# GeGLU feed-forward, first loads: x by quarters of D, the first two tiles of the weight chunk ahead of the others on two queues, four banks held instead of six

## The chip, the cores and the metric

One core of one Trainium2 chip. The metric is device time in microseconds (us), from several executions of each kernel. TensorE does the matmuls and transposes and writes them to PSUM, which this kernel uses as eight banks; ACT and DVE copy the results on; loads are issued on the queues of SP and of ACT.

## The reference

```python
B, S, D, F = 1, 2048, 1024, 3584      # bf16
def reference(x, w_gate, w_up, w_down):
    return (gelu_tanh(x @ w_gate) * (x @ w_up)) @ w_down
```

## The kernel before

The kernel keeps all weights' chunks and activations in SBUF and works in phases: a start phase of plain units for the first chunk of four tiles (128 bf16 matmuls of 128x512), then pairs of tiles with a seven-product scheme (12.6 us a pair), then the down projection, and the pairs and the down projection once more for the second half of the rows. The change concerns the start phase alone: how the first 512 rows of x and the first chunk of w_gate and w_up get in, and in which order TensorE uses them.

```python
    XQ = 512
    NXQ = D // XQ
    KPQ = XQ // P
    WKP = 2
    NSU = 3
    NWARM = 11
# ...
    def load_w(key, k0, k1, eng):
        c0 = key[1] * FG
        for w_sb, wv in zip(chunks[key], (wgv, wuv)):
            i = eng.dma_start(out=w_sb[:, k0:k1, :], in_=wv[:, k0:k1, c0 : c0 + FG])
            if eng is nc.sync:
                sp(i)
# ...
    new_chunk((0, 0))
    load_x0_piece(0)
    load_w((0, 0), 0, WKP, nc.scalar)
    nc.scalar.preload_act_table(ACT.Gelu_apprx_tanh)
    ident = const_pool.tile([P, P], BF16, name="ident")
    make_identity(nc, ident[:])

    warm_l = nc.const_aps.tensor(1.0, [P, P], BF16)
    warm_r = nc.const_aps.tensor(1.0, [P, TB], BF16)
    warm = []
    for i in range(NWARM):
        b = banks[i % 8]
        warm.append(
            nc.tensor.matmul(b[:], lhsT=warm_l, rhs=warm_r, start=True, stop=True)
        )

    load_x0_piece(1)
    for k0 in range(WKP, KD, WKP):
        load_w((0, 0), k0, k0 + WKP, nc.sync)
    load_xT(xT, 0, 1, 0, KD)
    new_chunk((0, 1))
    load_w((0, 1), 0, KD, nc.sync)
# ...
    def first_units(hT):
        groups = [warm, transpose_x_piece(0)]
        held = [(banks[2 + 2 * u], banks[3 + 2 * u]) for u in range(NSU)]
        bank_ctr[0] = 0
        for kd in range(KD):
            if kd == KPQ - 1:
                bank_ctr[0] = 0
                groups.append(transpose_x_piece(1))
            g = []
            for j, w_sb in enumerate(chunks[(0, 0)]):
                g += [mm_gu(held[u][j], w_sb, u, 0, kd) for u in range(NSU)]
            groups.append(g)
        for ga, gb in zip(groups[:-1], groups[1:]):
            tc.add_manual_dep(
                gb[0].ins, ga[-1].ins.name, SCHED_DEP, reason="startup PE order"
            )
        t_sum("t1")
        for u in range(NSU):
            mult(hT, gelu(held[u][0]), held[u][1], u, 0)
```

In words: x's first block comes as two halves of 512 columns on the SP queue; the first gate and up rows come on the ACT queue, the rest on SP. TensorE fills the time with eleven matmuls on constants, transposes one half of x, works on three tiles at once (six PSUM banks held), transposes the other half and goes on. `on`, `sp`, `act`, `dve`, `pe` are helpers that fix the order of instructions on an engine.

Of the kernel before, what the change touches and what calls it, by code (L numbers as in the profile page):

```python
# [8 lines left out]
ACT = mybir.ActivationFunctionType  # L9
# [25 lines left out]
def kernel(  # L35
# [23 lines left out]
    DN = 512  # L59
    NDN = D // DN  # L60
    TSB = TB // P
    XQ = 512
    NXQ = D // XQ
    KPQ = XQ // P
    WKP = 2
    NSU = 3
    NWARM = 11
    NPAIR = KF // 2
    PPG = FPG // 2
    WDT = 2  # L70
# [36 lines left out]

    banks = [psum.tile([P, TB], F32, name=f"bank{i}") for i in range(8)]
    PB, VB, QB, RB = (0, 1), (2, 3), (4, 5), (6, 7)
    bank_ctr = [0]  # L110

    def next_bank():
        b = banks[bank_ctr[0] % 8]
        bank_ctr[0] += 1
        return b

    last_on = {}

    def on(engine, inst):
# [8 lines left out]
    def sp(inst):  # L128
        return on("sp", inst)

    def act(inst):
        return on("act", inst)

    def dve(inst):
        return on("dve", inst)
# [12 lines left out]
    def pe(inst):  # L148
        return on("pe", inst)
# [11 lines left out]
            for j in range(2)  # L161
        )

    def load_w(key, k0, k1, eng):
        c0 = key[1] * FG
        for w_sb, wv in zip(chunks[key], (wgv, wuv)):
            i = eng.dma_start(out=w_sb[:, k0:k1, :], in_=wv[:, k0:k1, c0 : c0 + FG])  # L167
            if eng is nc.sync:
                sp(i)

    def load_x0_piece(q):
        sp(
            nc.sync.dma_start(
                out=xs0[:, :, q * XQ : (q + 1) * XQ],
                in_=x2[0:TB, q * XQ : (q + 1) * XQ].rearrange(
                    "(ts p) d -> p ts d", p=P
                ),
            )
        )

    def load_xT(xT, h, tb, k0, k1):
        t0 = h * SH + tb * TB
# [6 lines left out]

    xT = xT_pool.tile([P, KD, SH], BF16, name="xT")  # L190
    new_chunk((0, 0))
    load_x0_piece(0)
    load_w((0, 0), 0, WKP, nc.scalar)
    nc.scalar.preload_act_table(ACT.Gelu_apprx_tanh)
    ident = const_pool.tile([P, P], BF16, name="ident")
    make_identity(nc, ident[:])

    warm_l = nc.const_aps.tensor(1.0, [P, P], BF16)
    warm_r = nc.const_aps.tensor(1.0, [P, TB], BF16)
    warm = []  # L200
    for i in range(NWARM):
        b = banks[i % 8]
        warm.append(
            nc.tensor.matmul(b[:], lhsT=warm_l, rhs=warm_r, start=True, stop=True)
        )

    load_x0_piece(1)
    for k0 in range(WKP, KD, WKP):
        load_w((0, 0), k0, k0 + WKP, nc.sync)
    load_xT(xT, 0, 1, 0, KD)  # L210
    new_chunk((0, 1))
    load_w((0, 1), 0, KD, nc.sync)


    tsum = {}
# [25 lines left out]


    def mm_gu(ps, w_sb, fi, tb, kd):
        return nc.tensor.matmul(  # L244
            ps[:],
            lhsT=w_sb[:, kd, fi * P : (fi + 1) * P],
            rhs=xT[:, kd, tb * TB : (tb + 1) * TB],
            start=(kd == 0),
            stop=(kd == KD - 1),
        )  # L250

    g_ctr = [0]
# [19 lines left out]
            )  # L272
        )

    def unit(hT, key, fi, tb):
        pss = (next_bank(), next_bank())
        for ps, w_sb in zip(pss, chunks[key]):
            for kd in range(KD):
                mm_gu(ps, w_sb, fi, tb, kd)
        mult(hT, gelu(pss[0]), pss[1], key[1] * FPG + fi, tb)  # L280

    evac_ctr = [0]

    def evac(dst, src):
        if evac_ctr[0] % 2 == 0:
            dve(nc.vector.tensor_copy(out=dst, in_=src))
        else:
            act(nc.scalar.copy(out=dst, in_=src))
        evac_ctr[0] += 1

    def transpose_x_piece(q):
        kds = list(range(q * KPQ, (q + 1) * KPQ))
        parts = []
        if q == 0:
            parts = [([kds[0]], (0, 2)), ([kds[0]], (2, 4)), ([kds[1]], (0, 4))]
            kds = kds[2:]
        parts += [(kds[i : i + 2], (0, 4)) for i in range(0, len(kds), 2)]
        insts = []
        for kd_list, (ts0, ts1) in parts:
            n = (ts1 - ts0) * P  # L300
            tp = next_bank()[:].bitcast(BF16)
            for j, kd in enumerate(kd_list):
                for ts in range(ts0, ts1):
                    c = j * n + (ts - ts0) * P
                    insts.append(
                        nc.tensor.transpose(  # L306
                            tp[:, c : c + P],
                            xs0[:, ts, kd * P : (kd + 1) * P],
                            ident[:],
                        )  # L310
                    )
            k0 = kd_list[0]
            evac(
                xT[:, k0 : k0 + len(kd_list), ts0 * P : ts1 * P],
                tp[:, 0 : len(kd_list) * n].rearrange("p (a b) -> p a b", b=n),
            )
        return insts

    def first_units(hT):
        groups = [warm, transpose_x_piece(0)]  # L320
        held = [(banks[2 + 2 * u], banks[3 + 2 * u]) for u in range(NSU)]
        bank_ctr[0] = 0
        for kd in range(KD):
            if kd == KPQ - 1:
                bank_ctr[0] = 0
                groups.append(transpose_x_piece(1))
            g = []
            for j, w_sb in enumerate(chunks[(0, 0)]):
                g += [mm_gu(held[u][j], w_sb, u, 0, kd) for u in range(NSU)]
            groups.append(g)  # L330
        for ga, gb in zip(groups[:-1], groups[1:]):
            tc.add_manual_dep(
                gb[0].ins, ga[-1].ins.name, SCHED_DEP, reason="startup PE order"
            )
        t_sum("t1")
        for u in range(NSU):
            mult(hT, gelu(held[u][0]), held[u][1], u, 0)
        bank_ctr[0] = 0


    ssum = {}
# [434 lines left out]
    for h in range(NH):  # L776
        hT = hT_pool.tile([P, KF, SH], BF16, name="hT")
        first_pair = 0
        if h == 0:
            first_units(hT)  # L780
            t_sum("t2")
            for fi in range(NSU, FPG):
                unit(hT, (0, 0), fi, 0)
            t_sum("b22")
            t_sum("t3")
            unit(hT, (0, 0), 0, 1)
            for name in S_NAMES:
                for j in range(2):
                    s_sum(0, PPG, j, name)
            t_sum("t4")  # L790
            for fi in range(1, FPG):
                unit(hT, (0, 0), fi, 1)
            first_pair = PPG
            xs = [(tb, kd) for tb in range(NTB) for kd in range(KD)]
            stage_load(0)
            stage_load(1)
        for pair in range(first_pair, NPAIR):
            if pair % PPG == 0 and (pair // PPG + 1) * PPG < NPAIR:
                key = (h, pair // PPG + 1)
                if key not in chunks:  # L800
                    new_chunk(key)
                    load_w(key, 0, KD, nc.sync)
            then = {}
            if h == 0:

# [44 lines left out]
        if h + 1 < NH:  # L850
# [7 lines left out]
            def w_fill(c, j):  # L858
                if j == 0:
                    new_chunk((nh, c))  # L860
                w_sb, wv = chunks[(nh, c)][j], (wgv, wuv)[j]
                for k0 in range(0, KD, KH):
                    src = wv[:, k0 : k0 + KH, c * FG : (c + 1) * FG]
                    sp(nc.sync.dma_start(out=w_sb[:, k0 : k0 + KH, :], in_=src))

            def s_fill(j, *names):
                for name in names:
# [60 lines left out]
```

## Time and profile before

| | before |
|---|---|
| median of the first three runs | 545.26 us (544.74 to 545.34) |
| span of the profiled run | 542.7 us |
| TensorE busy | 537.7 us, 99% |
| DVE, ACT, POOL busy | 64%, 48%, 45% |
| first useful instruction on TensorE (transpose) | 5.51 us |
| pairs start | 35.53 us |

How to read it: the list of TensorE's waits has none after 7.65 us, so the end is the start of the pairs plus 507.2 us. Two readings carry everything below. One is "transposes start": the first TensorE instruction that isn't a matmul on constants. The other is "pairs start": the first matmul of the line that holds the pairs' products (L396 in the kernel before, L380 in the changed one). Both are starts as the timeline gives them; from one execution to another of the same kernel they move by up to 0.2 us (e1, e9). A busy share says little here: the constants count as busy.

Two reading aids. The first is the pace of the array, read from the weight loads (PEld). In the kernel before, the loads of the constants start at 3.71, 4.14 and 4.57 us, 0.43 us apart; from 11.95 us on, 110 matmuls of 512 columns take 23.74 us, 0.22 each. "Half rate" and "full rate" stand here for these two paces, and "the switch" for the moment between them. The granted-clock column says 1.00 at both, also in the first 4 us. "Clock" is the word for this pace. The second: the lines of the two kernels have other numbers (L204 and L197 are the constants, L306 and L295 the transposes, L244 and L245 the units).

### The profile page before, as it was taken

The page shows a single profiled execution, that of the slowest core. Times are in us where ns is not written, and L with a number is a line of the kernel's source. Part 1 is how long each engine was busy: PE and PEld are TensorE (multiplying, and loading weights), DVE is VectorE, ACT ScalarE, POOL GpSimd, SP SyncE. Part 2 cuts the span into 40 slices and gives each one's busy share as a digit, 9 for nine tenths or more (in the row PEclk, how much of TensorE's full clock was granted, in tenths as well). Part 3 has the DMA queues.
Part 4 walks back from the last instruction along what each step waited for, and adds up shares of the span by engine and source line. Part 5 has one row for each costly group of instructions (what it writes and reads, how often), then busy time and mean ns, then how long its engine had stood idle before and what let it go on. Part 6 is the DMA issues. An engine that isn't in the chain of part 4 may idle for free.

```text
span 542.7 us, 7261 instructions
## 1 busy us (share of the span) xinstructions
PE 537.7 (99%) x2411; PEld 374.1 (69%) x2411; DVE 349.5 (64%) x465; ACT 259.8 (48%) x434; POOL 242.2 (45%) x206
## 2 busy tenths in 40 slices
PE   8999999999999999999999999999999999999997
PEld 4456677777767676767777766777766776866865
DVE  1826666778766899789484444444454469979961
ACT  2435555555555318216455555555555552462270
POOL 0577777888877000000038776677777630000000
PEclk9999999999999999999999999999999999999999
DMA  9845598877736979679962240404040457767845
GB/s 275 267 133 155 162 241 278 216 252 194 252 137 213 335 246 367 215 245 307 320 213 80 76 129 27 155 2 156 0 156 0 156 171 238 251 219 246 289 146 206
DMA packets 81669, 104.82 MB, mean 193 GB/s; under 512 B 16608, under 2 KB 63200, under 8 KB 81632
## 3 DMA queue, kind: packets, MB, share of 16 engines
q1 hardware_dynamic: 81088, 103.83, 60.0%
q10 hardware_dynamic: 544, 0.52, 0.3%
q8 instruction: 20, 0.33, 0.2%
q14 instruction: 17, 0.14, 0.1%
HBM read 87.56 MB, written 13.63 MB: 186 GB/s over the span
## 4 chain that ended last, share of the span: by engine, by line
PE 98%; DMA 1%; ACT 0%; ACTq 0%; issue 0%
PE bank L396 60%; PE bank L632 32%; PE bank L244 5%; DMA w_mem<-in_w_up_dram 1%; PE bank L306 0%; ACT o_sb L680 0%; ACTq L167 0%; ACTq L680 0%
## 5 line engine op out<-in xcount | busy, mean ns | idle before, releaser
L396 PE MATMUL bank<-t_mem,s_mem 128*128 128x512 f32 x1016 | 249.2, 399 | 0.0
L396 PEld LDWEIGHTS bank<-t_mem,s_mem 128*128 128x128 f32 x1016 | 190.9, 188 | 44.2
L370 POOL TENSOR_TENSOR s_mem<-w_mem 128x512 fp32r<-128x512 bf16 x100 | 120.9, 1230 | 196.1 <-DVE t_mem L238 105.0
L632 PE MATMUL bank<-t_mem,s_mem 128*128 128x512 f32 x560 | 130.1, 392 | 0.0
L419 DVE TENSOR_TENSOR bank<-bank,m 128x512 f32<-128x512 f32 x104 | 72.3, 699 | 81.3 <-ACT bank L439 72.3
L632 PEld LDWEIGHTS bank<-t_mem,s_mem 128*128 128x128 f32 x560 | 105.2, 188 | 22.7
L267 DVE TENSOR_TENSOR hT<-w_mem,bank 128x512 bf16<-128x512 f32 x104 | 71.3, 688 | 54.4 <-ACT w_mem L262 24.6
L262 ACT ACTIVATE w_mem<-bank 128x512 f32<-128x512 f32 x104 | 61.9, 597 | 79.4 <-DVE bank L419 46.2
L396 PE MATMUL bank<-xT,w_mem 128*128 128x512 bf16 x416 | 99.0, 380 | 0.0
L396 PEld LDWEIGHTS <-w_mem 128*128 128x128 bf16 x416 | 36.6, 98 | 50.5 <-issue 13.6
L545 DVE TENSOR_TENSOR t_mem<-w_mem 128x1024 fp32r<-128x1024 bf16 x56 | 65.5, 1216 | 0.0
L370 POOL TENSOR_TENSOR s_mem<-w_mem,s_mem 128x512 fp32r<-128x512 bf16 x50 | 63.3, 1288 | 0.0
L370 POOL TENSOR_TENSOR s_mem<-s_mem,w_mem 128x512 fp32r<-128x512 f32 x50 | 59.3, 1206 | 0.0
L607 DVE TENSOR_TENSOR s_mem<-hT 128x512 fp32r<-128x512 bf16 x56 | 40.5, 754 | 10.5 <-PE bank L632 7.0
L383 ACT CAST s_mem<-w_mem 128x512 fp32r<-128x512 bf16 x52 | 31.9, 615 | 30.4 <-PE bank L396 29.2
L632 PEld LDWEIGHTS <-hT 128*128 128x128 bf16 x224 | 21.3, 98 | 26.6 <-issue 1.8
L434 ACT COPY m<-bank 128x512 f32<-128x512 f32 x52 | 30.6, 589 | 17.2 <-PE bank L396 17.0
L439 ACT COPY bank<-bank 128x512 f32<-128x512 f32 x52 | 29.6, 570 | 17.1 <-PE bank L396 17.1
L430 ACT COPY bank<-bank 128x512 f32<-128x512 f32 x52 | 29.5, 570 | 13.4 <-PE bank L396 13.4
L680 ACT CAST o_sb<-bank 128x512 bf16<-128x512 f32 x28 | 15.4, 586 | 39.6 <-PE bank L632 39.6
L244 PE MATMUL bank<-xT,w_mem 128*128 128x512 bf16 x128 | 28.1, 379 | 0.4 <-DMA w_mem<-in_w_up_dram 0.4
L542 ACT CAST t_mem<-w_mem 128x1024 fp32r<-128x1024 bf16 x28 | 26.9, 1048 | 0.0
(39 smaller groups left out, 233.4 us busy)
## 6 DMA issues: line engine op xcount, KB each, us to landing
t_mem<-t_dram SPq DMA_DIRECT2D x56, 512.0 KB, 5.5
w_mem<-in_w_gate_dram SPq DMA_DIRECT2D x11, 1024.0 KB, 6.2
w_mem<-in_w_up_dram SPq DMA_DIRECT2D x11, 1024.0 KB, 8.4
wd_sb<-in_w_down_dram SPq DMA_DIRECT2D x28, 256.0 KB, 3.4
t_dram<-o_sb SPq DMA_DIRECT2D x28, 256.0 KB, 2.5
wd_sb<-in_w_down_dram SPq DMA_DIRECT2D x12, 512.0 KB, 8.5
w_mem<-in_w_down_dram SPq DMA_DIRECT2D x10, 512.0 KB, 5.8
w_mem<-in_w_down_dram SPq DMA_DIRECT2D x4, 1024.0 KB, 6.8
```

The source lines that it names most:

```text
L244: return nc.tensor.matmul(ps[:], lhsT=w_sb[:, kd, fi * P : (fi + 1) * P], rhs=xT[:, kd, tb * TB : (tb + 1) * TB], start=(kd == 0), stop=(k ...
L262: act(nc.scalar.activation(out=g_sb, in_=ps[:], func=ACT.Gelu_apprx_tanh))
L267: nc.vector.tensor_tensor(out=hT[:, fc, tb * TB : (tb + 1) * TB], in0=g_sb, in1=ps[:], op=ALU.mult,)
L370: pool(nc.gpsimd.tensor_tensor(out=t, in0=in0, in1=in1, op=op))
L383: act(nc.scalar.copy(out=t, in_=a(1, 1)))
L396: nc.tensor.matmul(banks[bank][:], lhsT=lhs[:, c, :], rhs=rhs[:, c, :], start=start and c == 0, stop=c == KH - 1, skip_group_check=True,)
L419: nc.vector.tensor_tensor(out=banks[dst][:], in0=banks[src][:], in1=m5[j][:], op=ALU.add)
L434: act(nc.scalar.copy(out=m5[j][:], in_=banks[VB[j]][:]))
L439: act(nc.scalar.copy(out=banks[RB[j]][:], in_=banks[QB[j]][:]))
L545: dve(nc.vector.tensor_tensor(out=t, in0=in0, in1=in1, op=ALU.subtract))
L607: dve(nc.vector.tensor_tensor(out=t, in0=in0, in1=in1, op=op))
L632: nc.tensor.matmul(banks[bset[u]][:], lhsT=lhs(i, u), rhs=rhs(i), start=start and i == 0, stop=stop and i == NS - 1, skip_group_check=True,)
```

## The change

The intent: get TensorE to useful work earlier by making what the first transposes and matmuls need small, and by letting the rest follow at the pace of the work. Cut to its core:

```diff
-    XQ = 512
+    XQ = 256
     NXQ = D // XQ
     KPQ = XQ // P
     WKP = 2
-    NSU = 3
-    NWARM = 11
+    NWARM = 8
...
-    def load_w(key, k0, k1, eng):
+    def load_w(key, j, k0, k1, queue=sp, f0=0, f1=FG):
+
         c0 = key[1] * FG
-        for w_sb, wv in zip(chunks[key], (wgv, wuv)):
-            i = eng.dma_start(out=w_sb[:, k0:k1, :], in_=wv[:, k0:k1, c0 : c0 + FG])
-            if eng is nc.sync:
-                sp(i)
-
-    def load_x0_piece(q):
-        sp(
-            nc.sync.dma_start(
-                out=xs0[:, :, q * XQ : (q + 1) * XQ],
-                in_=x2[0:TB, q * XQ : (q + 1) * XQ].rearrange(
-                    "(ts p) d -> p ts d", p=P
-                ),
-            )
-        )
+        eng = nc.scalar if queue is act else nc.sync
+        src = (wgv, wuv)[j][:, k0:k1, c0 + f0 : c0 + f1]
+        queue(eng.dma_start(out=chunks[key][j][:, k0:k1, f0:f1], in_=src))
+
+    def load_x0(q, queue):
+        eng = nc.scalar if queue is act else nc.sync
+        cols = slice(q * XQ, (q + 1) * XQ)
+        src = x2[0:TB, cols].rearrange("(ts p) d -> p ts d", p=P)
+        queue(eng.dma_start(out=xs0[:, :, cols], in_=src))
...
-    load_x0_piece(0)
-    load_w((0, 0), 0, WKP, nc.scalar)
-    nc.scalar.preload_act_table(ACT.Gelu_apprx_tanh)
+
+    FA = 2 * P
+    first = (0, 0)
+    load_x0(0, sp)
+    load_w(first, 0, 0, 2, act, 0, FA)
+    load_w(first, 1, 0, 2, sp, 0, FA)
+    load_x0(1, act)
+    load_w(first, 0, 2, 4, sp, 0, FA)
+    load_w(first, 1, 2, 4, act, 0, FA)
+    act(nc.scalar.preload_act_table(ACT.Gelu_apprx_tanh))
     ident = const_pool.tile([P, P], BF16, name="ident")
     make_identity(nc, ident[:])
 
     warm_l = nc.const_aps.tensor(1.0, [P, P], BF16)
     warm_r = nc.const_aps.tensor(1.0, [P, TB], BF16)
-    warm = []
     for i in range(NWARM):
-        b = banks[i % 8]
-        warm.append(
-            nc.tensor.matmul(b[:], lhsT=warm_l, rhs=warm_r, start=True, stop=True)
+        pe(
+            nc.tensor.matmul(
+                banks[i][:], lhsT=warm_l, rhs=warm_r, start=True, stop=True
+            )
         )
 
-    load_x0_piece(1)
-    for k0 in range(WKP, KD, WKP):
-        load_w((0, 0), k0, k0 + WKP, nc.sync)
-    load_xT(xT, 0, 1, 0, KD)
+    for q in range(2, NXQ):
+        load_x0(q, sp)
+        for j in range(2):
+            load_w(first, j, 2 * q, 2 * q + 2, sp, 0, FA)
+    for j in range(2):
+        load_w(first, j, 0, KD, sp, FA, FG)
+    for k0 in range(0, KD, KH):
+        load_xT(xT, 0, 1, k0, k0 + KH)
     new_chunk((0, 1))
-    load_w((0, 1), 0, KD, nc.sync)
+    for j in range(2):
+        load_w((0, 1), j, 0, KD)
...
+    def transpose_x0(q):
+
+        parts = [(2 * q, 0, 4), (2 * q + 1, 0, 4)]
         if q == 0:
-            parts = [([kds[0]], (0, 2)), ([kds[0]], (2, 4)), ([kds[1]], (0, 4))]
-            kds = kds[2:]
-        parts += [(kds[i : i + 2], (0, 4)) for i in range(0, len(kds), 2)]
-        insts = []
-        for kd_list, (ts0, ts1) in parts:
-            n = (ts1 - ts0) * P
-            tp = next_bank()[:].bitcast(BF16)
-            for j, kd in enumerate(kd_list):
-                for ts in range(ts0, ts1):
-                    c = j * n + (ts - ts0) * P
-                    insts.append(
-                        nc.tensor.transpose(
-                            tp[:, c : c + P],
-                            xs0[:, ts, kd * P : (kd + 1) * P],
-                            ident[:],
-                        )
+            parts = [(0, 0, 2), (0, 2, 4), (1, 0, 4)]
+        for n, (kd, ts0, ts1) in enumerate(parts):
+            tp = banks[(PB + QB)[(2 * q + n) % 4]][:].bitcast(BF16)
+            for ts in range(ts0, ts1):
+                pe(
+                    nc.tensor.transpose(
+                        tp[:, ts * P : (ts + 1) * P],
+                        xs0[:, ts, kd * P : (kd + 1) * P],
+                        ident[:],
                     )
-            k0 = kd_list[0]
-            evac(
-                xT[:, k0 : k0 + len(kd_list), ts0 * P : ts1 * P],
-                tp[:, 0 : len(kd_list) * n].rearrange("p (a b) -> p a b", b=n),
-            )
-        return insts
+                )
+            cols = slice(ts0 * P, ts1 * P)
+            if n % 2 == 0:
+                dve(nc.vector.tensor_copy(out=xT[:, kd, cols], in_=tp[:, cols]))
+            else:
+                act(nc.scalar.copy(out=xT[:, kd, cols], in_=tp[:, cols]))
...
+        wg, wu = chunks[first]
+        held = (VB, RB)
+        transpose_x0(0)
+        for q in range(NXQ):
+            for kd in (2 * q, 2 * q + 1):
+                for u in range(2):
+                    mm_gu(banks[held[u][0]], wg, u, 0, kd)
+            for kd in (2 * q, 2 * q + 1):
+                for u in range(2):
+                    mm_gu(banks[held[u][1]], wu, u, 0, kd)
+                if kd == 2 * q and q + 1 < NXQ:
+                    transpose_x0(q + 1)
+        for u in range(2):
+            unit_out(hT, held[u], u, 0)
...
             first_units(hT)
+            unit(hT, PB, 2, 0)
+            t_sum("t1")
+            unit(hT, QB, 3, 0)
             t_sum("t2")
-            for fi in range(NSU, FPG):
-                unit(hT, (0, 0), fi, 0)
             t_sum("b22")
+            unit(hT, VB, 0, 1)
             t_sum("t3")
-            unit(hT, (0, 0), 0, 1)
             for name in S_NAMES:
                 for j in range(2):
                     s_sum(0, PPG, j, name)
+            unit(hT, RB, 1, 1)
             t_sum("t4")
-            for fi in range(1, FPG):
-                unit(hT, (0, 0), fi, 1)
+            unit(hT, QB, 2, 1)
+            unit(hT, VB, 3, 1)
```

More of the change, by code (lines that the diff above doesn't have):

```diff
@@ L109 @@
     PB, VB, QB, RB = (0, 1), (2, 3), (4, 5), (6, 7)
-    bank_ctr = [0]
-    def next_bank():
-        b = banks[bank_ctr[0] % 8]
-        bank_ctr[0] += 1
-        return b
     last_on = {}
@@ L243, in mm_gu @@
     def mm_gu(ps, w_sb, fi, tb, kd):
-        return nc.tensor.matmul(
-            ps[:],
-            lhsT=w_sb[:, kd, fi * P : (fi + 1) * P],
-            rhs=xT[:, kd, tb * TB : (tb + 1) * TB],
-            start=(kd == 0),
-            stop=(kd == KD - 1),
+        pe(
+            nc.tensor.matmul(
+                ps[:],
+                lhsT=w_sb[:, kd, fi * P : (fi + 1) * P],
+                rhs=xT[:, kd, tb * TB : (tb + 1) * TB],
+                start=(kd == 0),
+                stop=(kd == KD - 1),
+            )
         )
@@ L273, in mult, with unit_out, unit @@
         )
-    def unit(hT, key, fi, tb):
-        pss = (next_bank(), next_bank())
-        for ps, w_sb in zip(pss, chunks[key]):
+    def unit_out(hT, bset, fi, tb):
+        mult(hT, gelu(banks[bset[0]]), banks[bset[1]], fi, tb)
+    def unit(hT, bset, fi, tb):
+        for b, w_sb in zip(bset, chunks[first]):
             for kd in range(KD):
-                mm_gu(ps, w_sb, fi, tb, kd)
-        mult(hT, gelu(pss[0]), pss[1], key[1] * FPG + fi, tb)
-    evac_ctr = [0]
-    def evac(dst, src):
-        if evac_ctr[0] % 2 == 0:
-            dve(nc.vector.tensor_copy(out=dst, in_=src))
-        else:
-            act(nc.scalar.copy(out=dst, in_=src))
-        evac_ctr[0] += 1
@@ L291, in transpose_x_piece @@
-    def transpose_x_piece(q):
-        kds = list(range(q * KPQ, (q + 1) * KPQ))
-        parts = []
-        if q == 0:
-            parts = [([kds[0]], (0, 2)), ([kds[0]], (2, 4)), ([kds[1]], (0, 4))]
-            kds = kds[2:]
-        parts += [(kds[i : i + 2], (0, 4)) for i in range(0, len(kds), 2)]
-        insts = []
-        for kd_list, (ts0, ts1) in parts:
-            n = (ts1 - ts0) * P
-            tp = next_bank()[:].bitcast(BF16)
-            for j, kd in enumerate(kd_list):
-                for ts in range(ts0, ts1):
-                    c = j * n + (ts - ts0) * P
-                    insts.append(
-                        nc.tensor.transpose(
-                            tp[:, c : c + P],
-                            xs0[:, ts, kd * P : (kd + 1) * P],
-                            ident[:],
-                        )
-                    )
-            k0 = kd_list[0]
-            evac(
-                xT[:, k0 : k0 + len(kd_list), ts0 * P : ts1 * P],
-                tp[:, 0 : len(kd_list) * n].rearrange("p (a b) -> p a b", b=n),
-            )
-        return insts
@@ L319, in first_units @@
-    def first_units(hT):
-        groups = [warm, transpose_x_piece(0)]
-        held = [(banks[2 + 2 * u], banks[3 + 2 * u]) for u in range(NSU)]
-        bank_ctr[0] = 0
-        for kd in range(KD):
-            if kd == KPQ - 1:
-                bank_ctr[0] = 0
-                groups.append(transpose_x_piece(1))
-            g = []
-            for j, w_sb in enumerate(chunks[(0, 0)]):
-                g += [mm_gu(held[u][j], w_sb, u, 0, kd) for u in range(NSU)]
-            groups.append(g)
-        for ga, gb in zip(groups[:-1], groups[1:]):
-            tc.add_manual_dep(
-                gb[0].ins, ga[-1].ins.name, SCHED_DEP, reason="startup PE order"
-            )
-        t_sum("t1")
-        for u in range(NSU):
-            mult(hT, gelu(held[u][0]), held[u][1], u, 0)
-        bank_ctr[0] = 0
+                mm_gu(banks[b], w_sb, fi, tb, kd)
@@ new lines, in unit @@
+        unit_out(hT, bset, fi, tb)
+    def transpose_x0(q):
+        parts = [(2 * q, 0, 4), (2 * q + 1, 0, 4)]
+        if q == 0:
+            parts = [(0, 0, 2), (0, 2, 4), (1, 0, 4)]
+        for n, (kd, ts0, ts1) in enumerate(parts):
+            tp = banks[(PB + QB)[(2 * q + n) % 4]][:].bitcast(BF16)
+            for ts in range(ts0, ts1):
+                pe(
+                    nc.tensor.transpose(
+                        tp[:, ts * P : (ts + 1) * P],
+                        xs0[:, ts, kd * P : (kd + 1) * P],
+                        ident[:],
+                    )
+                )
+            cols = slice(ts0 * P, ts1 * P)
[3 more added lines that the diff above has]
+                act(nc.scalar.copy(out=xT[:, kd, cols], in_=tp[:, cols]))
@@ L801 @@
                     new_chunk(key)
-                    load_w(key, 0, KD, nc.sync)
+                    for j in range(2):
+                        load_w(key, j, 0, KD)
             then = {}
@@ L860, in w_fill @@
                     new_chunk((nh, c))
-                w_sb, wv = chunks[(nh, c)][j], (wgv, wuv)[j]
                 for k0 in range(0, KD, KH):
-                    src = wv[:, k0 : k0 + KH, c * FG : (c + 1) * FG]
-                    sp(nc.sync.dma_start(out=w_sb[:, k0 : k0 + KH, :], in_=src))
+                    load_w((nh, c), j, k0, k0 + KH)
             def s_fill(j, *names):
```

## The prediction

> **What bounds the kernel now.** I read the page's busy shares and chain first, then the waits of TensorE, then the chain in order of time, then the first microseconds as a timeline and as one-microsecond stretches. The chain that ended last, in order of time (start us, length us, what):
>
> ```profile
> 1.24 6.36 DMA w_mem<-in_w_up_dram
> 7.60 0.05 issue
> 7.65 3.41 PE bank L244 x15
> 11.06 0.89 PE bank L306 x16
> 11.95 23.74 PE bank L244 x110
> 35.70 151.35 PE bank L396 x672
> 187.05 87.89 PE bank L632 x392
> ...
> 539.32 0.59 ACT o_sb L680
> ```
>
> From 7.65 us to the last eviction everything on the chain is TensorE. The list of waits says the same: TensorE waits three times in the whole run, all before 7.65 us (start us is not in this view; the columns are who waited for what, total us, times, longest).
>
> ```profile
> PE bank L204 <- PEq L912: 0.8, 1, 0.8
> PE bank L244 <- DMA w_mem<-in_w_up_dram: 0.4, 1, 0.4
> PE bank L306 <- DMA w_mem<-in_x_dram: 0.3, 1, 0.3
> ```
>
> So a change of the start can only move the moment at which the real work begins and the holes before 7.65 us; whatever it saves there is carried unchanged to the end, and whatever it loses too. The start as a timeline of TensorE (start, us, line, operation, count, idle before):
>
> ```profile
> 0.77 4.42 PE L204 MATMUL bank<-const-bfloat16-1.0 128*128 128x512 bf16 x11 [0.77 <-PEq L912]
> 5.51 1.07 PE L306 MATMUL bank<-ident,w_mem 128*128 128x128 bf16 x16 [0.32 <-DMA w_mem<-in_x_dram]
> 6.41 0.82 PE L244 MATMUL bank<-xT,w_mem 128*128 128x512 bf16 x3
> 7.65 3.41 PE L244 MATMUL bank<-xT,w_mem 128*128 128x512 bf16 x15 [0.41 <-DMA w_mem<-in_w_up_dram]
> ```
>
> Eleven matmuls on constants fill the time to 5.19 us and compute nothing. The first useful instruction, a transpose of x, starts at 5.51. The phase of plain units (128 matmuls, 32 transposes) ends where the pairs start, 35.53 us. Its cost without any wait: in the chain 110 matmuls take 23.74 us, 0.2158 us each, and 16 transposes 0.89 us, 0.056 each; 128 x 0.2158 + 32 x 0.056 = 29.4 us. Measured: 35.53 - 5.51 = 30.0. The holes in it are thus 0.6 us, the rest is the start at 5.51.
>
> What the DMA brought meanwhile (stretch, length, busy of the engines, clock, DMA share, GB/s):
>
> ```profile
> 1.00:2.00 1.00, 1.00 (x3) 0.30 (x2) 0.00 (x0) 0.17 (x1) 0.29 (x1) 1.00 0.16 14
> 2.00:3.00 1.00, 1.00 (x4) 0.44 (x3) 0.00 (x0) 1.00 (x1) 0.00 (x0) 1.00 0.74 225
> 3.00:4.00 1.00, 1.00 (x4) 0.31 (x3) 0.00 (x0) 0.11 (x1) 0.00 (x0) 1.00 0.89 272
> 4.00:5.00 1.00, 1.00 (x4) 0.28 (x2) 0.00 (x0) 0.00 (x0) 0.00 (x0) 1.00 1.08 379
> 5.00:6.00 1.00, 0.68 (x10) 0.49 (x10) 0.17 (x1) 0.06 (x1) 0.00 (x0) 1.00 1.09 378
> ```
>
> Summed: 0.014 MB at 2 us, 0.24 at 3, 0.51 at 4, 0.89 at 5, 1.27 at 6. After that it stays near 350 GB/s. The first half of x (0.524 MB) and the first gate piece (0.262) make 0.786 MB, which the sum reaches at 4.7 us; the first transpose starts 5.51. I read 0.7 to 0.8 us from the last needed byte to its use.
>
> [...] its granted-clock column says 1.00 all along: weight loads of the constant matmuls come 0.43 us apart up to 4.57 us, twice 0.2158, and the eleventh ends at 5.19, so the switch came near 4.6 us. [...] No transfer of exactly 512 B rows is in this trace. The nearest is the DMA transpose, at 256 B a packet (0.87 MB over 3394 packets between 12 and 15 us):
>
> ```profile
> DMA packets 3394, 0.87 MB, mean 290 GB/s; under 512 B 3394, under 2 KB 3394, under 8 KB 3394
> ```
>
> [...]
>
> **The change part by part.** (a) x's first block comes as four pieces of 256 columns (0.262 MB) instead of two of 512; rows become 512 B instead of 1 KB. (b) The first weight pieces hold two of the four tiles (256 columns, 0.131 MB for two rows of blocks), on two queues; the other two tiles' columns come as 0.524 MB per matrix after them. (c) Transposes come eight at a time before each quarter. (d) Two tiles (four banks) are held instead of three (six banks). (e) 8 constant matmuls instead of 11. (f) The orders of the sums on DVE, ACT and POOL shift slightly. Counts of useful matmuls (128), transposes (32) and all pair and down work are unchanged: from 35.53 us on, nothing in the instructions of TensorE differs.
>
> When can transposes start? First needed bytes: x quarter plus the first gate piece on the other queue, 0.262 + 0.131 = 0.393 MB. The sum above reaches that at 3 + (0.393 - 0.239) / 0.272 = 3.57 us; plus 0.7 gives 4.3 us. The eight constant matmuls end at 0.77 + 8 x 0.427 = 4.19 us, so they are just out of the way. Gain of the start: 5.51 - 4.3 = 1.2 us. It cannot exceed 5.51 - 4.19 = 1.3.
>
> What holes come? First: in before, the first real matmul starts 0.90 us after the first transpose, exactly behind 16 transposes. The copy that it needs on ACT starts 0.43 us after the first transpose and lasts 0.37, so it is not ready before about 0.85 to 0.9 either way. With 8 transposes (0.45 us) TensorE now stands 0.45 us there. Then, at each of the three later quarters, two matmuls (0.43 us) separate the transposes from the first matmul on their result. The DVE copy of 512 columns takes 0.425 us; with 0.2 us from transpose to copy and 0.1 back, it is ready 0.22 + 0.2 + 0.43 + 0.1 = 0.95 us after the first transpose, wanted at 0.45 + 0.43 = 0.88. The ACT copy of the second half, about 0.6 us by interpolation between 0.37 (256 columns) and 1.01 (1024), is also within 0.05. I put 0.25 us in all on those. Before's holes of 0.6 us (0.41 of them for the first up piece) go. Half clock between 4.3 and 4.6 us costs up to 0.15.
>
> Is the DMA in time? One quarter is 8 transposes and 8 matmuls, 0.45 + 1.73 = 2.18 us, and needs 0.524 MB; at 350 GB/s that takes 1.5 us. Deadlines from 4.3: second x quarter at 6.5 us (0.92 MB with what is ahead of it, there at 5.8), third at 8.7 (1.31 MB, 6.8), last up piece of the held tiles at 12.6 (2.10 MB, 9.1), remaining gate columns at 4.3 + 0.45 + 1.8 + 6.9 = 13.4 (2.62 MB, 10.6), remaining up columns at 15.2 (3.15 MB, 12.1). The rates that would just meet them are 240, 209, 245 and 253 GB/s for the tight ones. So it needs about 250 GB/s with 512 B rows.
>
> The other engines: DVE begins its first difference at 15.96 us in before and ends the fourth at 28.6, wanted only late in the first pair; shifted by two extra multiplies it ends about 30.6. POOL's sums start with the arrival of the second chunk (20.24 us); the issue order before it has more entries but about the same 14 us. The first of them is ready at 26.4, wanted at about 36. No new wait there.
>
> Sum: 4.3 + 29.4 + 0.45 + 0.25 + 0.1 = 34.5 us for the start of the pairs, against 35.53: 1.0 us less. 545.26 - 1.0 = 544.3 us.
>
> **The rivals.** First, small rows: if 512 B rows run at only 200 GB/s, the last up columns come near 3.6 + 2.76 / 0.2 + 0.7 = 18.1 us against 15.2, a hole of 2.9 us, which is more than the start gains: 546 to 547. Against it stands the 290 GB/s with still smaller packets; for it, the share of DMA busy time there was 127%[...]. Second, clock: [...] the idle stretch between the eighth constant matmul and the first transpose may keep the array at half rate[...]: 545 to 546. Third, the start is set by first-byte latency: bytes came only at 2 us, and the x quarter shares the engines with everything behind it; with a landing at 5.0 the gain shrinks to 0.3 us: 545. Fourth, all goes perfectly and evictions hide: 1.5 us and no more, 543.7. A later engine (POOL or DVE) becoming late in the first pair I hold at under one in twenty.
>
> **Range and chances.** The ceiling is 1.5 us, 0.3%, and even the worst rival costs under 2 us; both are far inside 2%, which is 10.9 us. The three timings of before spread over 0.6 us. I centre on 544.3 and take 543.3 to 545.7 for 8 in 10, the upper side wider because three rivals lie there. Faster by over 2%: 0.5%; slower: 0.5%; within: 99%.
>
> **What would show it.** In the timeline of the changed kernel: transposes at about 4.3 us in four groups of eight, a hole of some 0.45 us before the first real matmul, no DMA wait on TensorE after 5 us, pairs from 34.5 us, and the same 504 us from there to the end. The DMA rate between 4 and 10 us should stay over 290 GB/s. It is wrong if TensorE waits for w_mem at 6 to 16 us (rows), if matmuls stand 0.43 us apart after 4.8 us (clock), or if transposes start at 5 us or later (latency).

4.3 + 29.4 + 0.45 + 0.25 + 0.1 came to 34.5 us for the start of the pairs, and 544.3 us in all. The second rival's 545 to 546 us stays as an estimate. One like it follows from the trace: half rate lasted from 0.77 to about 4.6 us, 3.8 us, and as long again would cost half of that, 1.9 us.

## The result

Over six runs each: 543.67 us median (543.39 to 544.56) against 545.12 (544.70 to 546.16). Ratio 0.9975, 95% interval 0.9963 to 0.9988. All outputs are right. The gain is 1.4 us in these rounds, far inside the 2% that a verdict of faster asks for; in a second call of five rounds with the same kernel (below) it was 0.9983, 0.9 us. The spans of the two profiled runs are 542.7 and 541.6 us, 1.1 apart.

The timeline of TensorE at the start of the changed kernel (start us, length us, engine, line, operation, count, idle before):

```profile
0.77 3.57 PE L197 MATMUL bank<-const-bfloat16-1.0 128*128 128x512 bf16 x8 [0.77 <-PEq L897]
4.33 1.03 PE L295 MATMUL bank<-ident,w_mem 128*128 128x128 bf16 x8
5.39 1.50 PE L245 MATMUL bank<-xT,w_mem 128*128 128x512 bf16 x6
6.73 0.61 PE L295 MATMUL bank<-ident,w_mem 128*128 128x128 bf16 x8
7.18 1.91 PE L245 MATMUL bank<-xT,w_mem 128*128 128x512 bf16 x8
8.93 0.61 PE L295 MATMUL bank<-ident,w_mem 128*128 128x128 bf16 x8
9.38 1.91 PE L245 MATMUL bank<-xT,w_mem 128*128 128x512 bf16 x7
11.12 0.61 PE L295 MATMUL bank<-ident,w_mem 128*128 128x128 bf16 x8
11.57 23.06 PE L245 MATMUL bank<-xT,w_mem 128*128 128x512 bf16 x104
34.47 1.89 PE L380 MATMUL bank<-xT,w_mem 128*128 128x512 bf16 x8
```

Transposes start at 4.33 instead of 5.51 us, in four groups of eight, and pairs at 34.47 instead of 35.53. A few matmul records are missing (7 and 104 stand for 8 and more). The list of waits of TensorE, for the whole run of the changed kernel, has one line left of three:

```profile
PE bank L197 <- PEq L897: 0.8, 1, 0.8
```

It is the wait for the program's own start, the same as before. From 0.77 to 4.33 us TensorE is now filled to the brim; that x, and not the constants, sets the 4.33 is seen on the weight loads, which wait for x while the last constant still runs. The second line below is ACT's copy of the second half of the first transposes, which the first real matmuls need:

```profile
4.32 0.77 PEld L295 LDWEIGHTS <-w_mem 128*128 128x128 bf16 x8 [0.88 <-DMA w_mem<-in_x_dram]
4.97 0.37 ACT L305 COPY xT<-bank 128x256 bf16<-128x256 bf16 x1 [1.30 <-PE bank L295]
```

What the DMA moved in the changed kernel (columns: stretch, length, the engines' busy shares, clock, DMA share, GB/s):

```profile
2.00:3.00 1.00, 1.00 (x4) 0.43 (x3) 0.00 (x0) 0.62 (x1) 0.00 (x0) 1.00 0.74 212
3.00:4.00 1.00, 1.00 (x4) 0.16 (x2) 0.00 (x0) 0.67 (x1) 0.00 (x0) 1.00 1.13 335
...
7.00:8.00 1.00, 1.00 (x11) 0.57 (x9) 0.42 (x1) 0.59 (x1) 0.00 (x0) 1.00 1.20 290
```

290 GB/s while the rows are 512 B, where the kernel before with its rows of 1 KB had 347 to 351 from 6 to 11 us: slower, and still enough. By these rates the 0.393 MB of x's first quarter and the first gate piece are there at 3.5 us (0.218 MB by 3 us, then 0.335 a microsecond), 0.8 us before the first transpose.

Where the 1.06 us came from, by the two timelines. The transposes start 1.18 us earlier. From the first transpose to the first real matmul it is 1.06 us now with 8 transposes in it (0.45 us of work) and was 0.90 with 16 (0.89): 0.60 us of new hole. (The timeline's 1.03 us for the eight transposes is a modelled end.) From the first real matmul to the pairs it is 29.08 us with 24 transposes, against 29.12 with 16; the work in them at 0.2158 and 0.056 us is 28.97 and 28.52, so the holes there shrank from 0.60 to 0.11. In sum: -1.18 + 0.60 - 0.49 = -1.07.

### The profile page after: what moved, and what is told of

Same layout as the page of the kernel before. It is cut to its first block, busy times and chain, and to the rows that moved or that the text cites. A ratio compares the mean times of both kernels' runs of the same rounds, so it can differ in the third digit from the quotient of the medians. Undisturbed runs are those within 1.5% of the kernel's fastest.

```text
span 541.6 us, 7230 instructions
## 1 busy us (share of the span) xinstructions
PE 535.2 (99%) x2371; PEld 374.1 (69%) x2408; DVE 351.3 (65%) x467; ACT 259.3 (48%) x435; POOL 242.3 (45%) x206
## 4 chain that ended last, share of the span: by engine, by line
PE 99%; issue 0%; ACT 0%; ACTq 0%
PE bank L380 60%; PE bank L616 32%; PE bank L245 5%; PE bank L197 1%; PE bank L295 0%; ACT o_sb L664 0%; ACTq L664 0%
## 5 line engine op out<-in xcount | busy, mean ns | idle before, releaser
L354 POOL TENSOR_TENSOR s_mem<-w_mem 128x512 fp32r<-128x512 bf16 x100 | 119.4, 1213 | 194.8 <-DMA w_mem<-in_w_up_dram 104.3
L380 PE MATMUL bank<-xT,w_mem 128*128 128x512 bf16 x390 | 95.5, 380 | 1.5
L354 POOL TENSOR_TENSOR s_mem<-s_mem,w_mem 128x512 fp32r<-128x512 f32 x50 | 61.2, 1244 | 0.0
L418 ACT COPY m<-bank 128x512 f32<-128x512 f32 x52 | 30.6, 588 | 17.1 <-PE bank L380 17.0
L245 PE MATMUL bank<-xT,w_mem 128*128 128x512 bf16 x125 | 28.2, 379 | 0.2
```

The costliest lines, as they stand in the source:

```text
L245: nc.tensor.matmul(ps[:], lhsT=w_sb[:, kd, fi * P : (fi + 1) * P], rhs=xT[:, kd, tb * TB : (tb + 1) * TB], start=(kd == 0), stop=(kd == KD ...
L354: pool(nc.gpsimd.tensor_tensor(out=t, in0=in0, in1=in1, op=op))
L380: nc.tensor.matmul(banks[bank][:], lhsT=lhs[:, c, :], rhs=rhs[:, c, :], start=start and c == 0, stop=c == KH - 1, skip_group_check=True,)
L418: act(nc.scalar.copy(out=m5[j][:], in_=banks[VB[j]][:]))
```

## The experiments

Three theories stood against each other. The first: the start is set by the bytes that arrive before x's first piece is complete, and the gain is their reduction. The second: it is set by the constants, three of which were dropped. The third: the switch of the array to full rate, which does not come at the same moment in every trace (from about 3.8 us in e6 to 10.3 in e3), makes or eats the gain. Twelve kernels ran, all timed in five to six rounds against the kernel before. The rivals of single runs are in their expectations. In this table "x" is the start of the transposes, "pairs" the start of the pairs in the one profiled execution, the first of each kernel's; in e3, e8 and e10 it was also the slowest. The three groups are three calls, each with its own runs of the kernel before (medians 544.61, 544.75 and 544.95 us).

| run | x, us | pairs, us | median, us | ratio to before (95%) |
|---|---|---|---|---|
| e1 changed, again | 4.54 | 34.63 | 543.67 | 0.9983 (0.9970 to 0.9997) |
| e2 changed, 11 constants | 4.93 | 34.80 | 544.41 | 0.9987 (0.9975 to 1.0000) |
| e3 changed, 4 constants | 4.33 | 36.79 | 545.90 | 1.0014 (1.0002 to 1.0027) |
| e4 before, 8 constants | 5.50 | 36.62 | 545.54 | 1.0015 (1.0002 to 1.0027) |
| e5 x by halves | 5.19 | 35.08 | 544.09 | 0.9990 (0.9976 to 1.0005) |
| e6 weights of all four tiles | 5.01 | 34.89 | 544.07 | 0.9988 (0.9976 to 1.0001) |
| e7 one queue | 4.14 | 34.30 | 543.04 | 0.9964 (0.9952 to 0.9976) |
| e8 x's first piece on both queues, 7 constants | 3.68 | 35.80 | 544.93 | 0.9996 (0.9982 to 1.0011) |
| e9 one queue, again | 4.07 | 34.26 | 543.56 | 0.9978 (0.9967 to 0.9990) |
| e10 one queue, 7 constants | 3.71 | 34.74 | 543.49 | 0.9970 (0.9959 to 0.9982) |
| e11 one queue, weights of all four tiles | 4.14 | 35.56 | 544.24 | 0.9993 (0.9978 to 1.0009) |
| e12 before, one queue | 5.28 | 35.71 | 544.83 | 0.9999 (0.9987 to 1.0011) |

In every row but e8 the span of the profiled execution is the pairs' start plus 506.8 to 507.6 us: what happens at the start passes through to the end, but for a scatter of 0.8 us. Two parts of the change had no run of their own and stay open: the two tiles held at once instead of three, and the order of the transposes among the matmuls. Undoing one of the other parts moved the pairs back by 0.2 to 0.3 us (e2, constants), 0.45 to 0.6 (e5, size of x's pieces) and 0.3 to 0.4 (e6, width of the weight pieces), of 1.06 us in all.

### e1: the changed kernel again

No edit.

> The changed kernel once more, unaltered, as the yardstick of this chip. Theory (transposes start 1.2 us earlier, the rest is carried through): 543.7 us, ratio to the kernel before 0.9975, transposes from 4.3 us, pairs from 34.5 us. Rival (the gain of 1.4 us in the medians is partly luck of the clock's switching moment): the ratio moves to 0.998 or above, and the trace shows the switch at another moment than about 5.2 us.

The same median, 543.67. The ratio came out at 0.9983, because the kernel before was lower on this chip; with the 0.9975 the timed gain is 0.9 to 1.4 us, and the prediction's 1.0 lies in it. x's first quarter came 0.2 us later than in the first profile (4.54 against 4.33), so part of the scatter is the arrival of the data. Half of the rival came true: the ratio is over 0.998. The other half did not: the switch to full rate was again near 5.3 us (six weight loads from 5.37 us take 1.19 us). e2, e6, e9 and e10, with about 4.5, 3.8, 4.0 and 6.7 us, show that it does wander.

### e2: constants

```diff
-    NWARM = 8
+    NWARM = 11
```

(and the bank index modulo 8.)

> The changed kernel with 11 constant matmuls again instead of 8. Theory (early data pays only because TensorE is free when it lands): the constants end near 5.1 us, transposes start there and not at 4.3, the hole before the first real matmul is 0.9 instead of 1.06 us, pairs from 35.1 us: 0.6 to 0.7 us slower than the changed kernel, about 544.3. Rival (the three constants are irrelevant, the earlier bytes alone carry the gain): no change, 543.7. Rival (eight are too few for the clock, which costs the changed kernel something): 11 are faster.

In this execution the array switched to full rate at about 4.5 us (weight loads at 4.14, 4.49 and 4.71), so that the last constants ran at full rate. Transposes follow them at 4.93, not 5.1, and as the array is at full rate by then, the first real matmul comes 0.85 us after the first of them instead of 1.06. Pairs are at 34.80, only 0.17 us later than e1's and 0.33 later than in the first profile. The medians differ by 0.7 us but the ratios, 0.9987 and 0.9983, don't separate. So the direction of the theory is seen in the timeline, its size isn't shown in the time.

### e3: too few constants

```diff
-    NWARM = 8
+    NWARM = 4
```

> The changed kernel with 4 constant matmuls: TensorE stands still from 2.5 to 4.3 us. If the idle time keeps the array at half rate (clock rival of the prediction): matmuls 0.43 us apart well past 5.4 us, pairs from 35.5 to 36.5 us, 1 to 2 us slower than the changed kernel. If the constants do nothing for the clock: pairs from 34.5, same time.

Pairs at 36.79, 2.3 us later than in the changed kernel, and the median 2.2 us higher. The timeline says why:

```profile
4.33 1.04 PE L295 MATMUL bank<-ident,w_mem 128*128 128x128 bf16 x8 [1.69 <-DMA w_mem<-in_x_dram]
5.40 2.72 PE L245 MATMUL bank<-xT,w_mem 128*128 128x512 bf16 x6
7.91 1.06 PE L295 MATMUL bank<-ident,w_mem 128*128 128x128 bf16 x8
8.76 2.65 PE L245 MATMUL bank<-xT,w_mem 128*128 128x512 bf16 x8
11.25 0.61 PE L295 MATMUL bank<-ident,w_mem 128*128 128x128 bf16 x8
```

The data came at the same moment, 4.33 us. But six matmuls and eight transposes take from 5.40 to 8.76 us, where the changed kernel needs 5.39 to 7.18; only the group at 11.25 has the short 0.61 us. The array stayed at half rate until about 10.3 us: weight loads at 9.19, 9.62 and 10.04, then three within 0.53 us from 10.39. This shows the cost of half rate alone: after 1.7 us of standing still came over 2 us of delay by it. The times bear it out: the spans of all five executions, 542.9 to 544.1 us, lie above all five of e1, 541.5 to 542.4.

### e4: eight constants in the kernel before

```diff
-    NWARM = 11
+    NWARM = 8
```

> The kernel before with 8 constant matmuls instead of 11, nothing else. Theory (its start waits for the half of x, which lands at about 5.5 us): transposes still from 5.5 us, pairs from 35.5, 545.1 us, or a little slower if the 1.3 us of standing still delays the clock. Rival (dropping constants is what gained): pairs from about 34.7, 0.8 us faster.

Transposes still start at 5.50, and the kernel gets slower: pairs at 36.62 instead of 35.53, ratio 1.0015. The longest wait of TensorE in this run:

```profile
PE bank L306 <- DMA w_mem<-in_x_dram: 1.2, 1, 1.2
```

After the 1.2 us between the eighth constant and the data the switch to full rate came only at about 8.9 us (weight loads at 7.61, 8.03 and 8.49, then five within 1.04 us from 8.88). So dropping constants alone isn't the gain, it's a loss; it is worth doing only together with earlier data. The second theory falls as a cause of its own.

### e5: x by halves again

```diff
-        cols = slice(q * XQ, (q + 1) * XQ)
+        cols = slice(q * XQ, (q + 2) * XQ)
...
-    load_x0(1, act)
...
-        load_x0(q, sp)
+        if q % 2 == 0:
+            load_x0(q, sp)
```

> The changed kernel with x in two loads of 512 columns on the SP queue instead of four of 256; weights, order of the work and 8 constants as changed. Theory (the start is set by the bytes ahead of the first transpose): 0.524 + 0.131 = 0.655 MB must come first, by the rates of the changed kernel at about 4.4 us, plus 0.7: transposes from about 5.1 us, 0.8 us later, pairs from about 35.2, time 544.4. Rival (latency of the first bytes sets the start, not their number): transposes from 4.3, no change.

Transposes at 5.19 (expected 5.1), pairs at 35.08 (expected 35.2), median 544.09: 0.4 us above e1's, where 0.7 had been expected; the intervals overlap. The trace carries it: the piece size of x (with its second quarter moved from the ACT to the SP queue, which the edit couldn't part from it) is worth 0.65 to 0.86 us in the start of the transposes, and 0.45 to 0.6 in the pairs. It loses less at the pairs because the first real matmul follows 0.86 us after the first transpose, at full rate. TensorE stood still for 0.85 us before the data here and in e6, and yet the eight transposes took their 0.45 us. In e4 it stood still for 1.15 us after the same eight constants and then ran at half rate for over 3 us. So a stop does not always cost half rate; what decides isn't shown by these runs.

### e6: weight pieces of all four tiles

```diff
-    FA = 2 * P
+    FA = FG
-    for j in range(2):
-        load_w(first, j, 0, KD, sp, FA, FG)
```

> The changed kernel with weight pieces of all four tiles (512 columns, rows of 1 KB, twice the bytes a piece) instead of two tiles ahead of the others; x in quarters as changed. Theory: the start moves little (4.3 to 4.5 us), but each quarter now needs 0.79 MB, 2.4 us at about 330 GB/s against 2.2 us of TensorE's work, so TensorE waits for data at the quarters: pairs 0.3 to 1.2 us later than 34.5. Rival (the two tiles ahead of the others are not needed): same as changed. The rate between 5 and 10 us should rise from 290 toward 350 GB/s if the narrow rows are what lowered it.

The expectation had the place wrong. There is no wait at the quarters; but x's first quarter itself came at 5.01 instead of 4.33 or 4.54. What differs by then is the gate piece beside it on the other queue, twice as large, and the pieces behind it. On one queue the same widening (e11 against e7) did not move the start (the weight loads had x at about 3.7 us in both), which speaks for the other queue's piece as the cause. But counting that piece whole explains only part: 0.524 MB were there at 4.0 us by e6's rates (0.203 MB by 3 us, then 314 GB/s), plus 0.7 gives 4.7. After that TensorE waits for nothing, with rates of 314 to 341 GB/s from 5 us on, where the changed kernel had 290: the rows of 1 KB were moved faster here, as the last sentence of the expectation had it. So on two queues loading two tiles ahead of the others helped by what it takes from x's first quarter, not by pacing the quarters.

### e7 and e9: one queue

```diff
-    load_w(first, 0, 0, 2, act, 0, FA)
+    load_w(first, 0, 0, 2, sp, 0, FA)
-    load_x0(1, act)
+    load_x0(1, sp)
-    load_w(first, 1, 2, 4, act, 0, FA)
+    load_w(first, 1, 2, 4, sp, 0, FA)
```

> The changed kernel with all first loads on the SP queue. If x's first quarter no longer shares the engines with the second queue, it lands somewhat earlier than 4.24 us, but the eight constants hold TensorE until 4.3, and the first gate piece is issued 0.5 us later. Theory: transposes from 4.3, the first real matmul not before 5.4, no later wait: within 0.3 us of changed. Rival (two queues are needed for issue time): waits for w_mem or x on TensorE after 5.4 us, up to 1 us slower.

> The one-queue variant once more, unaltered, on this call's chip. If it is really better than the changed kernel: 543.0 us and a spread under 0.4 us in five executions, transposes from 4.14 us, pairs from 34.3. If the first look was luck: 543.6 with a second group near 544.4, as the changed kernel had twice.

In e7 transposes start at 4.14, pairs at 34.30, the median is 543.04 and five executions lie within 0.24 us. That looked better than the changed kernel. The repeat, e9, had the same starts (4.07, 34.26) but a median of 543.56 and a spread of 0.8 us: the first was partly luck. The issues of the repeat on the SP queue (start, length, queue, line):

```profile
0.74 0.45 SPq L167 DMA_DIRECT2D w_mem<-in_x_dram  x1
...
3.87 0.47 SPq L167 DMA_DIRECT2D w_mem<-in_x_dram  x1
```

One issue takes about 0.5 us, so the pieces enter one after the other. No other queue moves anything beside x's first quarter, and it lands at about 3.7 us, before the eight constants end (the transposes follow them at 4.14 us in e7). The price is at the third quarter, whose issue comes only at 3.87: in e9 its transposes stand until 8.71 us, the weight loads waiting 0.64 us for x. Whether one queue is really better than two by the 0.2 to 0.4 us that the pairs show (34.30 and 34.26 against 34.47 and 34.63) isn't settled by the times: its two ratios, 0.9964 and 0.9978, and the changed kernel's, 0.9975 and 0.9983, have overlapping intervals.

### e8: both queues for x's first quarter

```diff
-    NWARM = 8
+    NWARM = 7
-    load_x0(0, sp)
+    for eng, q_, t0 in ((nc.sync, sp, 0), (nc.scalar, act, 2)):
+        src = x2[t0 * P : (t0 + 2) * P, 0:XQ]
+        src = src.rearrange("(ts p) d -> p ts d", p=P)
+        q_(eng.dma_start(out=xs0[:, t0 : t0 + 2, 0:XQ], in_=src))
```

> An attempt to go further: the first quarter of x as two token halves, one at the head of each queue, and 7 constants. If the bytes ahead of the first transpose are all that counts, 0.262 MB arrive 0.4 us earlier: transposes from about 3.9 us, pairs from about 34.1, 0.4 us faster than changed. If the clock still runs at half rate until about 5.2 us, the first matmuls are slow and eat most of it: gain 0.1 or nothing.

The first part worked: transposes at 3.68. Then the second quarter, issued on the ACT queue at 1.79 us, landed only at 8.0, 6.2 us later, with 0.262 MB:

```profile
PE bank L298 <- DMA w_mem<-in_x_dram: 2.0, 1, 2.0
PE bank L619 <- DMA t_mem<-t_dram: 1.0, 2, 0.5
```

The second line is a wait in the down projection that no other profile here shows; it added 1.0 us to this one execution. Pairs at 35.80, and the six executions spread over 2.8 us (543.40 to 546.15). The profiled one is the slowest of them, and the fastest has the span of the changed kernel's first profile, 541.6 us, so the late landing can't be taken for the rule. By the packets of the two queues, the changed kernel's ACT queue had moved its 0.52 MB by 6 us; here it moved 0.66 MB and was not done before 7. Why the ACT queue fell so far behind is not settled.

### e10: one queue, seven constants

```diff
-    NWARM = 8
+    NWARM = 7      # on top of e7
```

> One queue with 7 constants. In the one-queue variant x's first quarter landed at 3.74 us while the constants ran to about 4.15. If the constants are what now holds the start: transposes from about 3.8 us, pairs from about 33.95, 0.3 to 0.4 us faster (542.7). If the clock, which switched only near 5.3 us in two of the traces, is what counts: the slow first matmuls eat it, gain under 0.2[...].

Transposes at 3.71, as expected, and still pairs at 34.74. The start of TensorE:

```profile
0.77 3.15 PE L197 MATMUL bank<-const-bfloat16-1.0 128*128 128x512 bf16 x7 [0.77 <-PEq L897]
3.71 1.06 PE L295 MATMUL bank<-ident,w_mem 128*128 128x128 bf16 x8
4.80 2.37 PE L245 MATMUL bank<-xT,w_mem 128*128 128x512 bf16 x6
7.01 0.61 PE L295 MATMUL bank<-ident,w_mem 128*128 128x128 bf16 x8
```

From 4.80 to 7.01 us are six matmuls, 2.21 us where full rate would take 1.29. In this execution, the slowest of the five, the switch to full rate came only near 6.7 us (weight loads 0.43 us apart up to 6.47, eight within 0.65 us from 6.80), although TensorE stood still only for about 0.2 us, behind the transposes. So useful work that starts earlier ran, in part, at half rate, and the 0.4 us that the start gained on e7 and e9 became a loss of 0.4 us at the pairs in this trace. In the times it is 543.49 against e9's 543.56, with 542.89 as the best. The slowest execution, the profiled one with its late switch, took 543.83.

### e11: one queue, weight pieces of all four tiles

> One queue, weight pieces of all four tiles (rows of 1 KB). With two queues this lost 0.4 us, all of it because x's first quarter came late (5.0 us); TensorE waited for nothing later. Theory (what counts is only what shares the engines with x's first quarter): on one queue nothing shares, so transposes from 4.1 to 4.2 us, no wait after, 543.0 to 543.2. Rival (two tiles ahead of the others are needed for the quarters to keep up, 0.79 MB a quarter): waits for w_mem at the second or third quarter, pairs 0.3 us or more later than 34.3.

Edits of e6 and e7 together. The theory fell, the rival was right: transposes started at 4.14, as on one queue, and then x came late at every quarter. The weight loads, with the idle time before them:

```profile
7.38 0.45 PEld L293 LDWEIGHTS <-w_mem 128*128 128x128 bf16 x8 [0.63 <-DMA w_mem<-in_x_dram]
...
9.83 0.45 PEld L293 LDWEIGHTS <-w_mem 128*128 128x128 bf16 x8 [0.57 <-DMA w_mem<-in_x_dram]
```

At the last quarter it is 0.49 us, at 12.20. Pairs at 35.56, 1.3 us later than e7 and e9. Quarters come every 2.4 us, which is 0.79 MB at 330 GB/s, instead of every 2.2. On two queues (e6) the same bytes caused no such wait; there the start was 0.9 us later, and the loads were issued on two queues. Which of the two made the difference no run tells. But on one queue the two tiles ahead of the others do earn their place in the trace: with them no such wait is left in e7, and only the one at the third quarter in e9. In the times e11 and e9 don't separate (0.9978 to 1.0009 against 0.9967 to 0.9990).

### e12: the kernel before on one queue

```diff
-    load_w((0, 0), 0, WKP, nc.scalar)
+    load_w((0, 0), 0, WKP, nc.sync)
```

> The kernel before with its two loads of the ACT queue moved to the SP queue, between the halves of x; 11 constants, halves and six banks as before. Theory (the bytes of the second queue delay x's first half, and the wait for the first up piece goes too): transposes at about 5.0 to 5.1 us, as the constants end, no wait at 7.65, pairs from about 34.9: 0.6 us faster than the kernel before. Rival (the halves are too large whatever the queue): transposes still from 5.4 us or later, 545.

No gain: ratio 0.9999. In this execution the switch to full rate came only near 5.1 us (the eleven constants last 4.67 us, 4.42 in the kernel before), inside the last of the constants, so the transposes came at 5.28 behind them; and a gate piece behind x's second half came late:

```profile
PE bank L244 <- DMA w_mem<-in_w_gate_dram: 0.5, 1, 0.5
```

It is the wait at 9.65 us; pairs start at 35.71. With pieces as large as these, moving them to one queue only moves the wait.

## Why the prediction was right

**The bound.** It held: nothing but the start of the pairs moved. From the pairs to the end the trace has 507.17 us before and 507.13 after, and the span shrank by as much as the pairs' start came forward (1.1 and 1.06). The prediction's 504 us for this stretch is short: from 35.53 us to the last eviction at 539.91 it is 504.4, and the span goes on to 542.7.

**When the transposes start.** Predicted 4.3, measured 4.33 (4.54 in the second profile). x was what they waited for, as said, but only just: with x earlier (e7) they start at 4.14, right behind the eight constants. The method, counting the bytes that must have arrived and adding 0.7 us, gave 5.1 for e5, where 5.19 was measured. Where it failed is e6: 4.3 to 4.5 was said, 5.01 came. The expectation had left the method out: with the whole gate piece counted it gives 4.7, and the other 0.3 us stay open.

**The holes.** Predicted: 0.45 before the first real matmul, 0.25 at the later quarters, 0.1 net for half rate, 0.80 in all. Measured: 0.61 and 0.11, 0.72 in all. The errors cancel. The first is larger, because the eight transposes ran at half rate (0.86 us in place of 0.45, up to about 5.2 us), so that the ACT copy of the second half began 0.64 us after the first transpose instead of the 0.43 read from before. The later ones are smaller. Where the transposes ran at full rate (e2, e5, e6, e9) the first real matmul came 0.85 to 0.86 us after the first of them instead of 1.06. So half rate cost 0.2 us here, not 0.1, and in another place than said: inside the wait for the copies.

**The DMA in time.** The prediction needed 250 GB/s with 512 B rows and expected over 290. Measured 289 to 294 between 5 and 12 us, and no wait after the first matmul. The inference from the DMA transposes' 290 GB/s was right; that the two figures agree to the last digit is not explained by any run. The same loads with weight rows of 1 KB ran at 314 to 341 GB/s (e6), and the kernel before, with rows of 1 KB throughout, had 347 to 351 from 6 to 11 us; so on two queues the wider rows came faster. On one queue the narrow rows reached 334 GB/s from 5 to 6 us (e7, 0.33 MB in 679 packets), so their width is not all of it. The size of the pieces is not it: from 9.3 us on what comes in the changed kernel is the two pieces of 0.524 MB, twice e6's 0.262 MB, still with 512 B rows, at 289 to 292 GB/s.

**Other engines.** Here a term was mis-sized, without effect on the time. The second chunk's first load was said to be issued near 14 us as before; it was issued at 15.64, since there are more issues ahead of it and the two DMA transposes took 7.3 us together instead of 6.0. POOL's first sums were ready at 28.3 us instead of 26.4. They are wanted at 36.0, so 7.7 us of slack remained, and TensorE waited for none of them. DVE's fourth difference ended at 31.5; 30.6 had been said.

**The rivals.** Small rows didn't bite. Half rate cost 0.2 us in the profiled executions of the changed kernel, but e3 and e4 show that it can cost more: the pairs came 2.3 us later in e3's trace, after 1.7 us of standing still before the data, and 1.1 us later in e4's, after 1.2. e10 shows a late switch without such a stop. By the weight loads and the length of the constants, the switch to full rate came at about 3.8 us (e6), 4.0 (e9), 4.5 (e2), 4.6 (before), 5.1 (e12), 5.3 (changed) and 6.7 (e10), with no stop of over 0.2 us before it; after the stops of 1.2 and 1.7 us it came at about 8.9 (e4) and 10.3 (e3). Late first bytes showed as 0.2 us between two executions of the same kernel. The full 1.5 us were not reached in the trace.

**What the times say.** 1.4 and 0.9 us, against 1.06 in the trace. The executions of the changed kernel scatter by 1.2 and 1.3 us, so 0.3 us either way has no cause that these runs could name. The recorded spans are the steadier measure: in the second call their medians are 541.7 us (five executions) against 542.8 (nine), 1.1 us apart as in the trace, and one execution took 544.57 us with a span of only 541.7, so part of the scatter lies outside the span. The wandering of the switch to full rate is a candidate for that scatter; it is argued from single traces, not shown over executions.

## What to carry to other kernels

Where one engine is busy from the first data to the end, as TensorE is here with no wait after 7.65 us, what is left to gain at the start is the moment of its first useful instruction: count the bytes that arrive before that moment, on all queues, and make them small. Fill the time before it with work that ends just as the data lands: too little left the array at half rate here (2 us in e3, 1 in e4, nothing in e5 and e6), too much delayed the real work (0.2 to 0.3 us in e2). Measure such changes by landmarks in the trace and by the spans of several executions, for a gain of 0.2% is as large as the scatter of the times.
